# A fused attention backward pass on one core: block-end transposes behind the dK products, VectorE's block-end work behind its 32x32 transposes, and the dQ copy on VectorE

## The chip, the cores and the metric

The kernel runs on one core of one Trainium2 chip. The metric is device time in microseconds (us) for one execution. Each kernel was timed in several runs, on the same chip as runs of the kernel before, and every comparison uses fast runs only: those within 1.5% of the kernel's fastest. The engine names are those of the profile: PE does the matrix products, PEld loads their weights, DVE is VectorE, ACT is ScalarE, POOL is GpSimd. A trace line such as "L720 ACT ACTIVATE eT<-sps" is the instruction of line 720 of that kernel on ScalarE, reading the tensor `sps` and writing `eT`.

## The reference

The reference returns the output of two attention blocks and all gradients of their inputs. Nearly all the time that matters here goes to block B, multi-query attention with 16 heads of 28 channels over 2,048 tokens, one shared K and V:

```python
def _B_ref(x, wq, wk, wv, wo):
    ...
    q = (x @ wq) -> (B, H, S, Dh);  k = x @ wk;  v = x @ wv       # shortened
    scores = einsum("bhqd,bkd->bhqk", q, k) * Dh ** -0.5
    p = softmax(scores, axis=-1)
    o = einsum("bhqk,bkd->bhqd", p, v)
    return o.transpose(...).reshape(B, S, H * Dh) @ wo

def reference(..., grad_out):
    out, vjp = jax.vjp(forward, ...)      # forward = concat(block A, block B)
    return (out, *vjp(grad_out))
```

## The kernel before

The core of the kernel is one loop over 512 *units*. A unit is 256 keys by 256 queries for two heads; 8 units make a *block* (all keys for one query chunk and two heads), and there are 64 blocks. Forward and backward are interleaved: in iteration `u`, PE makes the scores of unit `u`, the gradients of the probabilities of unit `w = u-16`, the output products of unit `v = u-1`, the dQ products of unit `y = u-18`, and the dK products of a block that began 28 units ago. All engines run the program in this order, each its own instructions.

```python
psS = tile_pool("psS", bufs=3, space=PSUM)    # score buffers, name "sps"
psD = tile_pool("psD", bufs=2, space=PSUM)    # gradient buffers, name "dps"
oq     = psA.tile([P, 512], F32, name="oq")   # columns 0:256: O in rows 0:64, dQ in rows 64:128
dk_acc = psA.tile([P, 512], F32, name="dk_acc")
...
for u in range(NU + 28):
    sp = [psS.tile([P, 512], F32, name="sps") for _ in range(2)]
    dp = [psD.tile([P, 512], F32, name="dps") for _ in range(2)]
    rows_SD(u, sp, dp)                        # PE: scores, gradients (four 32-row groups side by side)

    nc.scalar.activation(et[:, u % 2, 0, :], sp[0], Exp, scale)              # L710 "first exponential"
    nc.vector.tensor_tensor(dst[:, 0, :], dp[0], ew[:, w % 2, 0, :], mult)   # L715 VectorE's product
    nc.scalar.activation(cp, dp[1], Copy)                                    # L717
    nc.gpsimd.tensor_tensor(dst[:, 1, :], cp, ew[:, w % 2, 1, :], mult)      # L718
    nc.scalar.activation(et[:, u % 2, 1, :], sp[1], Exp, scale)              # L720 "second exponential"
    ...
    if (u - 9) % 8 == 0:     # block end, unit 1 of a block (cut)
        onp = psS.tile([P, 2, 2, 32], F32, name="sps")
        nc.tensor.transpose(onp..., oTs[b]...)                               # L731
        nc.vector.reciprocal(r_, onp[..., 0:1])                              # L740
        nc.vector.tensor_tensor(onat..., onp, r_, mult)                      # L744
        ...
    if (u - 14) % 8 == 0:    # unit 6
        tp2 = psS.tile([P, 1024], BF16, name="sps")
        nc.tensor.transpose(tp2..., don[b]...)                               # L776
        nc.vector.tensor_copy(doT[b]..., tp2...)                             # L780
    # dK products of block (u-28)//8: 12 matmuls a unit, 8 in two units, none in two
    # output products (v) and dQ products (y) into oq; dV products in units 2 and 3
    ...
    if u % 64 in (16, 24) and u > 64:
        out_proj(...)        # four products into a score buffer, copied out by VectorE
    if v % 8 == 7:           # unit 0
        nc.vector.tensor_copy(oTs[v // 8], oq[0:64, 0:256])                  # L844
    if y % 8 == 7:           # unit 1: the dQ copy
        nc.scalar.activation(qT_B..., oq[64:128, 0:256], Copy, scale)        # L847
    nc.vector.transpose(dsx[b][:, tp]..., dsT[y]...)                         # L853, 32x32 transposes
```

Three score buffers serve two scores a unit, so the buffers rotate: a score product can start when the last reader of the buffer that it is given is done. Which buffer a tile gets is settled when the program is built. Mostly it is the one used three allocations earlier. The block-end transposes take a turn in the same rotation, and there it depends on the order of the program around them: at unit 7 of this kernel the second score tile gets the buffer of the transpose just before it, which the `doT` copy frees.

## Time and profile before

| | before |
|---|---|
| median of 3 runs, ahead of the prediction | 1173.73 us (1172.52 to 1174.92) |
| span of the profiled run | 1172.0 us |
| ordinary block (41 of blocks 8 to 62), median | 12.78 us |
| block with an output projection (14 of them), median | 13.74 us |
| first exponential to first exponential, units 0 to 7 of an ordinary block | 1.458, 2.026, 1.457, 1.519, 1.458, 1.545, 1.811, 1.506 us |
| second exponential to next first, unit 1 to 2 and unit 6 to 7 | 1.056 us and 0.841 us |

A block is measured from the start of its first exponential to that of the next block. A unit needs at least 1.458 us on ScalarE; what a unit takes above that is what there is to win or lose.

The first line of the page, busy time of each engine over the whole span:

```profile
PE 1099.7 (94%) x15388; PEld 444.6 (38%) x15388; DVE 885.5 (76%) x1669; ACT 900.9 (77%) x1788; POOL 699.4 (60%) x835
```

PE looks like the limit. The groups of instructions of ScalarE between 400 and 1000 us say otherwise (columns: line, engine, operation, tensors, shapes, count, then busy us and mean ns, then idle time just before and what ended it):

```profile
L720 ACT ACTIVATE eT<-sps 128x512 bf16<-128x512 f32 x369 | 224.8, 609 | 0.0
L710 ACT ACTIVATE eT<-sps 128x512 bf16<-128x512 f32 x369 | 221.5, 600 | 18.1 <-PE dps L591 16.6
...
L847 ACT ACTIVATE R_63<-oq 64x256 bf16<-64x256 f32 x46 | 17.4, 379 | 5.0 <-PE oq L591 4.1
```

The Trainium skill, "Trainium Kernel Development and Optimization", Performance Expectations, warns of just this reading of matmul busy time, and here the warning holds. In 600 us ScalarE is idle for about 23 us. Its instructions are the pace, and the first exponential is the only one that waits to speak of. The passage from unit 1 to unit 2, in the timeline (columns: start us, length us, then the instruction):

```profile
676.32 0.62 ACT L720 ACTIVATE eT<-sps 128x512 bf16<-128x512 f32 x1
...
676.66 0.59 PE L591 MATMUL sps<-R_63,R_65 32*128 32x256 bf16 x2
...
676.96 0.38 ACT L847 ACTIVATE R_63<-oq 64x256 bf16<-64x256 f32 x1
...
677.00 0.36 PE L591 MATMUL sps<-R_63,R_65 32*128 32x256 bf16 x2
...
677.37 0.60 ACT L710 ACTIVATE eT<-sps 128x512 bf16<-128x512 f32 x1
```

The dQ copy ends at 677.34, and the last score product of unit 2 ends at 677.36. The copy and the scores are ready at the same moment, 1.05 us after the second exponential began. The scores are late because their buffer is the one that the second exponential reads until 676.94.

The passage from unit 6 to unit 7, in the timeline of the same kernel:

```profile
683.45 0.27 PE L776 MATMUL sps<-identB,don 128*64 128x128 bf16 x2
...
683.95 0.27 DVE L780 COPY doT<-sps 64x256 bf16<-64x256 bf16 x1
684.15 0.69 DVE L853 STREAM_TRANSPOSE dsx<-dsT 128x512 f32<-128x512 f32 x1
684.32 0.60 ACT L720 ACTIVATE eT<-sps 128x512 bf16<-128x512 f32 x1
...
684.74 0.28 PE L591 MATMUL sps<-R_63,R_65 32*128 32x256 bf16 x2
...
685.16 0.60 ACT L710 ACTIVATE eT<-sps 128x512 bf16<-128x512 f32 x1 [0.24 <-PE dps L591]
```

Here the score products of unit 7 start at 684.74, while the second exponential still runs (to 684.92): they do not need its buffer. The `doT` copy, ahead of VectorE's 32x32 transpose, has freed theirs by 684.22. The step is 0.84 us, and it is PE's queue that sets it.

The waits of PE between 400 and 1000 us show one wait for VectorE (columns: instruction and what it waited for, us in total, times, longest):

```profile
PE sps L731 <- DVE oTs L844: 8.2, 12, 0.7
```

### The profile page before, as it was taken

What the parts mean: (1) busy time and instruction counts of PE and PEld (TensorE: products, weight loads), DVE (VectorE), ACT (ScalarE), POOL (GpSimd) and SP (SyncE); (2) the same over time, 40 slices, a digit from 0 to 9 for tenths busy, and PEclk for the clock granted to TensorE, in tenths of its full rate; (3) what the DMA queues carried; (4) which work ended last, traced back from release to release, by engine and by line L of the source; (5) the groups of instructions that cost most, each with busy time, mean ns of one, the idle gap of its engine ahead of it and who ended that gap; (6) DMA issues with size and microseconds to landing.
All of it is one profiled execution on the core that took longest, in us unless ns stands there. A gap on an engine that the chain in (4) does not pass through costs nothing. (4 is left out here: it accounts for less than half of the span.)

```text
span 1172.0 us, 38434 instructions
## 1 busy us (share of the span) xinstructions
PE 1099.7 (94%) x15388; PEld 444.6 (38%) x15388; DVE 885.5 (76%) x1669; ACT 900.9 (77%) x1788; POOL 699.4 (60%) x835
## 2 busy tenths in 40 slices
PE   7999997988989999999999999999999999999998
PEld 4555543333333333333333333333333333333344
DVE  7886400336889898888889888988999899888922
ACT  3453112357989999999999999999999999999511
POOL 9000150003777777777778777877787778777900
PEclk9999998989999999999999999999999999999999
DMA  9779897059999999999999999999999999999962
GB/s 259 126 130 184 160 188 177 20 125 198 180 179 190 188 164 187 190 184 175 189 188 160 199 188 186 162 198 188 152 195 182 189 170 199 184 168 163 240 147 75
DMA packets 684435, 202.91 MB, mean 173 GB/s; under 512 B 651232, under 2 KB 679392, under 8 KB 684256
## 3 DMA queue, kind: packets, MB, share of 16 engines
q1 hardware_dynamic: 673664, 190.26, 94.8%
q10 hardware_dynamic: 9312, 6.65, 2.1%
q0 software_dynamic: 1280, 3.55, 1.1%
q8 instruction: 120, 1.97, 0.7%
q14 instruction: 59, 0.48, 0.1%
HBM read 22.83 MB, written 15.03 MB: 32 GB/s over the span
## 5 line engine op out<-in xcount | busy, mean ns | idle before, releaser
L718 POOL TENSOR_TENSOR dsT<-cp,eT 128x512 bf16<-128x512 bf16 x512 | 590.3, 1153 | 193.2 <-ACT cp L717 156.2
L715 DVE TENSOR_TENSOR dsT<-dps,eT 128x512 bf16<-128x512 f32 x512 | 347.8, 679 | 58.3 <-PE dps L591 37.6
L853 DVE STREAM_TRANSPOSE dsx<-dsT 128x512 f32<-128x512 f32 x512 | 357.8, 699 | 1.3 <-POOL dsT L718 0.3
L710 ACT ACTIVATE eT<-sps 128x512 bf16<-128x512 f32 x512 | 307.3, 600 | 42.2 <-PE dps L591 28.3
L591 PEld LDWEIGHTS <-R_65 32*128 32x128 bf16 (+1 forms) x8192 | 171.5, 92 | 403.3 <-issue 356.1
L717 ACT ACTIVATE cp<-dps 128x512 bf16<-128x512 f32 x512 | 305.1, 596 | 12.0 <-PE dps L591 11.1
L720 ACT ACTIVATE eT<-sps 128x512 bf16<-128x512 f32 x512 | 311.6, 609 | 0.0
L591 PE MATMUL dk_acc<-dsx,qX 32*32 32x512 bf16 x4096 | 290.4, 377 | 0.0
L591 PE MATMUL dps<-doT,R_65 32*128 32x256 bf16 x2048 | 253.9, 271 | 7.7 <-DVE R_64 L824 1.1
L591 PE MATMUL sps<-R_63,R_65 32*128 32x256 bf16 x2048 | 242.9, 276 | 5.9 <-ACT eT L710 2.0
L591 PE MATMUL oq<-eT,R_65 128*32 128x256 bf16 x2048 | 213.8, 278 | 2.5 <-issue 0.3
L591 PE MATMUL oq<-dsT,R_65 128*32 128x256 bf16 x2048 | 203.1, 278 | 1.1 <-POOL dsT L718 0.9
L591 PEld LDWEIGHTS <-qX 32*32 32x32 bf16 x4096 | 69.4, 89 | 94.1 <-issue 54.1
L591 PE MATMUL dv_acc<-eN,don 128*32 128x512 bf16 x1024 | 86.9, 382 | 2.5 <-DMA eN<-eT 2.5
L521 DVE TENSOR_TENSOR osb<-R_65 32x512 bf16<-32x512 bf16 x4 | 1.7, 413 | 74.2 <-ACT R_65 L518 74.2
L380 POOL MEMSET ga<- 64x448 bf16 x2 | 0.9, 468 | 90.8 <-PE agen L337 71.3
L553 POOL MEMSET R_65<- 128x16 bf16 x1 | 0.2, 172 | 70.8 <-DVE R_65 L552 70.8
L748 POOL TENSOR_TENSOR don<-R_64,rl 128x128 bf16<-128x128 bf16 x64 | 25.8, 403 | 21.4 <-DVE rl L740 21.4
L844 DVE COPY oTs<-oq 64x256 f32<-64x256 f32 x64 | 26.5, 414 | 15.1 <-PE oq L591 14.4
L731 PE MATMUL sps<-identF,oTs 64*128 64x64 f32 x128 | 21.3, 247 | 17.0 <-DVE oTs L844 10.6
L591 PEld LDWEIGHTS <-don 128*32 128x32 bf16 x1024 | 34.7, 97 | 4.0 <-issue 3.9
L79 PEld LDWEIGHTS <-R_64 128*128 128x128 bf16 x256 | 23.9, 100 | 28.0 <-issue 10.3
(216 smaller groups left out, 961.2 us busy)
## 6 DMA issues: line engine op xcount, KB each, us to landing
qX<-qn_d SPq DMA_DIRECT2D x128, 64.0 KB
out_dram<-osb ACTq DMA_DIRECT2D x44, 112.0 KB
eN<-eT SPq DMA_TRANSPOSE x256
qn_d<-dsx SPq DMA_DIRECT2D x1, 2048.0 KB
on_d<-onat SPq DMA_DIRECT2D x8, 256.0 KB
xa<-in_A_x_dram SPq DMA_DIRECT2D x8, 224.0 KB
ga<-in_grad_out_dram SPq DMA_DIRECT2D x4, 448.0 KB
xa<-in_grad_out_dram POOLq DMA_DIRECT2D x4, 448.0 KB, 4.7
```

Of the source, the lines that this page charges most:

```text
L79: nc.tensor.matmul(out_ap, lhsT=lhsT, rhs=rhs, start=start, stop=stop, tile_position=(0, 0))
L521: nc.vector.tensor_tensor(out=sq[0:32, :], in0=kT[0:32, qc * 512:(qc + 1) * 512], in1=kT[0:32, qc * 512:(qc + 1) * 512], op=ALU.mult)
L591: nc.tensor.matmul(out, lhsT=lhsT, rhs=rhs, start=start, stop=stop, tile_position=pos, skip_group_check=True)
L710: nc.scalar.activation(out=et[:, u % 2, 0, :], in_=sp[0][:, :], func=ACT.Exp, scale=scale)
L715: nc.vector.tensor_tensor(out=dst[:, 0, :], in0=dp[0][:, :], in1=ew[:, w % 2, 0, :], op=ALU.mult)
L717: nc.scalar.activation(out=cp[:, :], in_=dp[1][:, :], func=ACT.Copy)
L718: nc.gpsimd.tensor_tensor(out=dst[:, 1, :], in0=cp[:, :], in1=ew[:, w % 2, 1, :], op=ALU.mult)
L720: nc.scalar.activation(out=et[:, u % 2, 1, :], in_=sp[1][:, :], func=ACT.Exp, scale=scale)
L731: nc.tensor.transpose(onp[:, qb, :, :].rearrange("p h c -> p (h c)"), oTs[b][0:64, qb * P:(qb + 1) * P], identF[0:64, 0:64], tile_position ...
L748: nc.gpsimd.tensor_tensor(out=dn[:], in0=dnv, in1=r_[:].to_broadcast([P, 2, 2, 32]), op=ALU.mult)
L844: nc.vector.tensor_copy(out=oTs[v // 8][:, :], in_=oq[0:64, 0:256])
L853: nc.vector.transpose(out=dsx[b][:, tp, :, :, :].rearrange("p h t c -> p (h t c)").bitcast(F32), in_=dsT[y][:, :, :].rearrange("p h c -> p ...
```

## The change

The intent is to shorten three waits at block ends. PE runs the dK products first and the block-end transposes after them, so that it has work while their inputs come. VectorE puts the 32x32 transpose ahead of the block-end work, so that the pacing chain's buffers come free earlier. The dQ copy leaves ScalarE, the pacer. The diff moves the pieces into helper functions; the new order is its core:

```diff
 # PE
-    onat_T(b)      at u % 8 == 1    # the helpers' names are used for the moved code
-    don_T(b)       at u % 8 == 6
-    dK products
+    dk_units(u)
+    onat_T(b)      at u % 8 == 1
+    don_T(b)       at u % 8 == 6
     output and dQ products, dV products
 ...
 # VectorE (GpSimd's parts move with it)
-    reciprocal, normalisation       (u % 8 == 1, ahead of the projection's copy)
-    row sums                        (u % 8 == 4)
-    doT copy                        (u % 8 == 6)
-    oTs copy                        (u % 8 == 0)
     32x32 transpose
+    o_norm(b): reciprocal, normalisation
+    row_D(b):  row sums
+    don_copy(b)
+    oTs copy
+    dQ copy
 ...
-    nc.scalar.activation(out=qT_B[g][64 * hp:64 * hp + 64, qc * 256:(qc + 1) * 256],
-                         in_=oq[64:128, 0:256], func=ACT.Copy, scale=scale)
+    nc.vector.tensor_scalar(out=qT_B[g][64 * hp:64 * hp + 64, qc * 256:(qc + 1) * 256],
+                            in0=oq[64:128, 0:256], scalar1=scale, scalar2=None, op0=ALU.mult)
```

In the kernel after, the first exponential is L827, VectorE's product L832, ScalarE's gradient copy L834, GpSimd's product L835, the second exponential L837, the two block-end transposes L697 and L741, the `doT` copy L749, the 32x32 transpose L876, the `oTs` copy L893 and the dQ copy L896.

## The prediction

> **What bounds the kernel.** The loop over 512 units (8 units make a block, 64 blocks) fills about 840 of 1172 us. The page shows PE 94% busy, but the Trainium skill, "Trainium Kernel Development and Optimization", Performance Expectations, warns that matmul busy time is a bad metric since matmuls are pipelined; the timeline agrees: groups of four 0.28 us matmuls start 0.12 us apart. In the timeline ScalarE is the pacer: its three activations per unit follow each other start to start in 0.493, 0.477 and 0.488 us, 1.458 us a unit, and 8 x 1.458 = 11.66 of the 12.78 us of an ordinary block. The rest: 0.57 at unit 1 (dQ copy 0.41, and 0.15 before it), 0.35 at unit 6, 0.2 of small delays. Blocks with an output projection (14) take 13.74 us. VectorE is busy about 89% (stretches of the windows view), GpSimd waits for ScalarE (view of waits).
>
> **What the change does.** It removes the dQ copy (0.38 us, x64) from ScalarE, adds it to VectorE (about 0.42 us, as the similar oTs copy), lets PE run the dK products while the transposes' inputs come, and puts VectorE's block end one 32x32 transpose (0.62 us start to start) later.
>
> **Why I expect no gain.** PE is in order, and three score buffers rotate. After each block-end transpose the next unit's scores need the buffer of the second exponential.
> - Unit 1 to 2: the score matmul starts 0.05 us after that exponential ends (0.617 us long), and the next exponential follows about 0.38 us after that start: about 1.045 us from start to start. Today exponential plus dQ copy take 1.054. The copy sits in a gap that exists anyway: gain 0.01 us a block.
> - Unit 6 to 7: today the scores take the doT transpose's buffer, released by VectorE's early doT copy, and the step is 0.841 us. With that copy after the 32x32 transpose, the built program's waits show the scores of unit 7 waiting for the second exponential of unit 6 instead: about 0.995 us. Loss 0.15, and about 0.06 more at unit 7, where PE arrives late. The reordering on PE gains 0.1 us there, which this wait hides.
> - Output-projection blocks: VectorE runs late there (it waits 1.07 us for the projection). Its chain of projection copy, transpose, oTs, product, transpose, reciprocal, normalisation, dQ copy now ends about 0.9 us after today's dQ copy; PE's output products of unit 2 wait for it, and with them the scores of unit 3: about 0.65 us more a block.
>
> Sum (estimate from the durations above): 50 x 0.2 + 14 x 0.9 = 23 us, all on the pacing loop; I shade it slightly for gains I can't see.
>
> **Predicted: 1194 us, range 1178 to 1204.** Chances: faster 0.06, same 0.55, slower 0.39.
>
> **What would show it.** Ordinary block about 12.98 us (right) or under 12.6 (wrong). ScalarE's busy time falls by about 24 us but its idle time before the first exponential rises by more. The step unit 6 to 7 grows from 0.84 to about 1.0; unit 1 to 2 stays near 1.04. PE's wait for the oTs copy at the first transposes shrinks in ordinary blocks; waits for the dQ copy appear on PE in projection blocks. VectorE busy rises about 25 us.
>
> **What would make it wrong.** If the scores' release is faster than 0.05 us or PE arrives later than I think; if the earlier VectorE products release the gradient buffers so that ScalarE's small delays vanish (0.2 us a block, 13 us); if the dQ copy on VectorE is much shorter than 0.42 us.

## The result, and the profile after

Ratios here and below are taken from the fast runs of the same rounds; they are not quite the ratio of the medians that are quoted.

| | before | after |
|---|---|---|
| median of fast runs, 4 of each in the same rounds | 1174.33 us (1172.52 to 1181.33) | 1203.66 us (1202.06 to 1206.16) |
| ratio, 95% interval | | 1.0243 (1.021 to 1.0275): slower |
| span of the profiled run | 1172.0 us | 1200.7 us |
| ordinary block, median | 12.78 us | 13.01 us (mean 13.02) |
| projection block, median | 13.74 us | 14.61 us (mean 14.89) |
| unit 1 to 2, unit 6 to 7 | 1.056, 0.841 us | 1.054, 0.991 us |
| VectorE, ScalarE busy | 885.5, 900.9 us | 911.7, 883.9 us |

The work moved as meant. The first line of the page after:

```profile
PE 1100.5 (92%) x15388; PEld 440.8 (37%) x15388; DVE 911.7 (76%) x1733; ACT 883.9 (74%) x1724; POOL 701.6 (58%) x835
```

ScalarE does 64 instructions and 17 us less, and the kernel is slower. Its groups in the same 600 us tell where the time went:

```profile
L837 ACT ACTIVATE eT<-sps 128x512 bf16<-128x512 f32 x355 | 215.1, 606 | 0.0
L827 ACT ACTIVATE eT<-sps 128x512 bf16<-128x512 f32 x356 | 213.5, 600 | 56.3 <-PE sps L591 17.5 <-issue 16.5 <-PE dps L591 13.6
```

The idle time before the first exponential went from 18.1 to 56.3 us, and 355 units pass where 369 did. Unit 1 to 2 in the timeline after:

```profile
756.15 0.62 ACT L837 ACTIVATE eT<-sps 128x512 bf16<-128x512 f32 x1
...
756.30 0.28 PE L591 MATMUL sps<-R,R 32*128 32x256 bf16 x1
...
756.82 0.26 PE L591 MATMUL sps<-R,R 32*128 32x256 bf16 x1 [0.24 <-ACT eT L837]
...
757.04 0.42 DVE L896 TENSOR_SCALAR R<-oq 64x256 bf16<-64x256 f32 x1
...
757.21 0.60 ACT L827 ACTIVATE eT<-sps 128x512 bf16<-128x512 f32 x1 [0.44 <-issue]
...
757.52 0.29 PE L591 MATMUL oq<-eT,R 128*32 128x256 bf16 x2 [0.30 <-DVE R L896]
```

The copy is gone from ScalarE and the step is the same: the scores wait for the second exponential, start 0.05 us after its end, and the next exponential follows 0.39 us later. ("issue" means that the profile shows nothing that ended the idle time; the scores end at 757.19.) Unit 6 to 7 in the timeline after:

```profile
763.88 0.30 PE L741 MATMUL sps<-identB,don 128*64 128x128 bf16 x2
763.90 0.70 DVE L876 STREAM_TRANSPOSE dsx<-dsT 128x512 f32<-128x512 f32 x1
...
764.19 0.60 ACT L837 ACTIVATE eT<-sps 128x512 bf16<-128x512 f32 x1
...
764.44 0.67 PE L591 MATMUL sps<-R,R 32*128 32x256 bf16 x2
...
764.63 0.29 DVE L749 COPY doT<-sps 64x256 bf16<-64x256 bf16 x1
...
764.85 0.28 PE L591 MATMUL dps<-doT,R 32*128 32x256 bf16 x2
...
765.18 0.60 ACT L827 ACTIVATE eT<-sps 128x512 bf16<-128x512 f32 x1 [0.39 <-PE sps L591]
```

The first score group begins at 764.44 but takes 0.67 us, since one of its matmuls cannot start before the second exponential ends at 764.79; all behind it start at 764.85. PE reached the scores 0.25 us after the second exponential began, 0.17 us earlier than before (0.42), and that is of no use. PE takes its products strictly in order, as the Trainium skill, "TensorE: Matmul & The Clock Gate", Part 3, The mechanism, states (strict order of arrival), and this trace agrees: the gradient products, whose own waits were over by 764.30 (VectorE's product and ScalarE's copy of unit 6), start with the blocked scores at 764.85. The scores do not wait for the `doT` copy here, which ends only at 764.92.

Projection blocks have a larger loss. Before, timeline at units 1 to 3 of one of them:

```profile
703.49 0.38 ACT L847 ACTIVATE R_63<-oq 64x256 bf16<-64x256 f32 x1 [0.37 <-PE oq L591]
...
703.90 0.60 ACT L710 ACTIVATE eT<-sps 128x512 bf16<-128x512 f32 x1
...
703.92 0.29 PE L591 MATMUL oq<-eT,R_65 128*32 128x256 bf16 x2
...
705.36 0.60 ACT L710 ACTIVATE eT<-sps 128x512 bf16<-128x512 f32 x1
```

After, the timeline of the same block:

```profile
715.90 0.60 ACT L827 ACTIVATE eT<-sps 128x512 bf16<-128x512 f32 x1 [0.78 <-POOL dsT L835]
...
716.40 0.43 DVE L896 TENSOR_SCALAR R<-oq 64x256 bf16<-64x256 f32 x1
...
716.88 0.29 PE L591 MATMUL oq<-eT,R 128*32 128x256 bf16 x2 [1.06 <-DVE R L896]
...
718.08 0.60 ACT L827 ACTIVATE eT<-sps 128x512 bf16<-128x512 f32 x1 [0.60 <-PE dps L591]
```

The copy comes last in VectorE's queue at a block end, PE's output products wait 1.06 us for it, and unit 2 takes 2.18 us instead of 1.46 us. The waits of PE after, between 400 and 1000 us:

```profile
PE oq L591 <- DVE R L896: 22.0, 44, 1.1
PE sps L697 <- DVE oTs L893: 8.4, 11, 0.8
PE sps L591 <- ACT eT L837: 8.2, 34, 0.2
```

The first and the third line are new. The wait for the dQ copy is there in ordinary blocks too, 0.30 us each (at 757.52 in the trace above).

One more thing is new. In 4 of the 14 projection blocks PE runs at half its clock for 3.413 us, and those blocks take 15.6 us instead of 14.6. The windows view after, around one of them (columns: stretch, length, busy us with counts of PE, PEld, DVE, ACT and POOL, granted PE clock, DMA share, GB/s):

```profile
497.00:500.50 3.50, 1.66 (x38) 0.87 (x34) 3.40 (x8) 2.72 (x6) 1.87 (x3) 1.00 0.86 203
500.50:504.00 3.50, 3.50 (x48) 1.03 (x44) 2.60 (x5) 2.21 (x6) 2.39 (x3) 0.52 0.48 96
```

PE is busy for less than half of the stretch before the drop. Before, there is no such window in the loop between 311 and 1170 us.

The sum, from the two profiled runs: 41 ordinary blocks x 0.242 = 9.9 us; 10 projection blocks x 0.86 and 4 with a slow clock x 1.85, together 14 x 1.14 = 16.0 us; the first eight blocks +0.4; ahead of the loop -0.5; from block 63 to the end +2.9. That is 28.7 us, as the spans differ.

### The profile page after: what moved, and what is told of

Read it like the earlier page. It is cut to its first block, busy times and chain, and to the rows that moved or that the text cites. A ratio compares the mean times of both kernels' runs of the same rounds, so it can differ in the third digit from the quotient of the medians.

```text
span 1200.7 us, 38383 instructions
## 1 busy us (share of the span) xinstructions
PE 1100.5 (92%) x15388; PEld 440.8 (37%) x15388; DVE 911.7 (76%) x1733; ACT 883.9 (74%) x1724; POOL 701.6 (58%) x835
## 5 line engine op out<-in xcount | busy, mean ns | idle before, releaser
L835 POOL TENSOR_TENSOR dsT<-cp,eT 128x512 bf16<-128x512 bf16 x512 | 591.2, 1155 | 215.2 <-ACT cp L834 203.0
L832 DVE TENSOR_TENSOR dsT<-dps,eT 128x512 bf16<-128x512 f32 x512 | 353.1, 690 | 77.9 <-ACT eT L837 40.4
L827 ACT ACTIVATE eT<-sps 128x512 bf16<-128x512 f32 x512 | 307.0, 600 | 91.0 <-PE sps L591 35.3
L876 DVE STREAM_TRANSPOSE dsx<-dsT 128x512 f32<-128x512 f32 x512 | 358.7, 701 | 0.0
L591 PEld LDWEIGHTS <-R 32*128 32x128 bf16 (+1 forms) x8192 | 171.6, 93 | 407.1 <-issue 387.2
L834 ACT ACTIVATE cp<-dps 128x512 bf16<-128x512 f32 x512 | 304.2, 594 | 16.7 <-PE dps L591 16.7
L837 ACT ACTIVATE eT<-sps 128x512 bf16<-128x512 f32 x512 | 310.0, 606 | 0.0
L591 PE MATMUL dk_acc<-dsx,qX 32*32 32x512 bf16 x4096 | 293.8, 381 | 0.0
L591 PE MATMUL sps<-R,R 32*128 32x256 bf16 x2048 | 250.9, 277 | 22.3 <-ACT eT L837 11.7
L591 PE MATMUL dps<-doT,R 32*128 32x256 bf16 x2048 | 241.2, 274 | 5.1 <-DVE R L858 1.1
L591 PE MATMUL oq<-eT,R 128*32 128x256 bf16 x2048 | 212.7, 280 | 29.5 <-DVE R L896 29.1
L591 PE MATMUL oq<-dsT,R 128*32 128x256 bf16 x2048 | 205.3, 281 | 2.4 <-DVE R L896 1.8
L79 PEld LDWEIGHTS <-R 128*128 128x128 bf16 (+1 forms) x416 | 34.2, 99 | 36.3 <-issue 12.3
L718 POOL TENSOR_TENSOR don<-R,rl 128x128 bf16<-128x128 bf16 x64 | 25.9, 404 | 26.8 <-ACT eT L827 23.1
L79 PE MATMUL agen<-R,R 128*128 128x448 bf16 x128 | 29.8, 363 | 3.2 <-DVE pk L227 1.9
L697 PE MATMUL sps<-identF,oTs 64*128 64x64 f32 x128 | 21.4, 248 | 11.6 <-DVE oTs L893 10.7
```

The source lines that it names most:

```text
L79: nc.tensor.matmul(out_ap, lhsT=lhsT, rhs=rhs, start=start, stop=stop, tile_position=(0, 0))
L591: nc.tensor.matmul(out, lhsT=lhsT, rhs=rhs, start=start, stop=stop, tile_position=pos, skip_group_check=True)
L697: nc.tensor.transpose(onp[:, qb, :, :].rearrange("p h c -> p (h c)"), oTs[b][0:64, qb * P:(qb + 1) * P], identF[0:64, 0:64], tile_position ...
L718: nc.gpsimd.tensor_tensor(out=dn[:], in0=dnv, in1=r_[:].to_broadcast([P, 2, 2, 32]), op=ALU.mult)
L827: nc.scalar.activation(out=et[:, u % 2, 0, :], in_=sp[0][:, :], func=ACT.Exp, scale=scale)
L832: nc.vector.tensor_tensor(out=dst[:, 0, :], in0=dp[0][:, :], in1=ew[:, w % 2, 0, :], op=ALU.mult)
```

## The experiments

The theory T is that of the prediction: at unit 7 the rotation of the score buffers ties the scores to the second exponential; in projection blocks VectorE's late dQ copy holds PE. The main rivals are R1: only VectorE's added work counts, each of its microseconds costs one; and R2: what hurts is PE's new order. Twelve kernels ran besides the two, all of them compared with the kernel before on the same chip; three gave wrong outputs, as told there, and nine correct ones.

| run | ordinary block | projection block, median | span | median | ratio to before, 95% |
|---|---|---|---|---|---|
| before | 12.78 | 13.74 | 1172.0 | 1174 | |
| after | 13.01 | 14.61 | 1200.7 | 1203.66 | 1.0243 (1.021 to 1.0275) |
| a_dq_scalar | 12.98 | 13.95 | 1186.1 | 1187.53 | 1.0093 (1.0066 to 1.0121) |
| b_dq_vector | 13.02 (mean) | 14.39 | 1191.7 | 1195.14 | 1.0153 (1.0127 to 1.0179) |
| b_dk_first | 12.98 | 13.88 | 1183.7 | 1185.83 | 1.0091 (1.0046 to 1.0136) |
| b_block_end_late | 12.98 | 14.50 | 1193.2 | 1194.99 | 1.0175 (1.0127 to 1.0223) |
| b_dot_late | 12.98 | 13.89 | 1184.0 | 1188.44 | 1.0139 (1.0097 to 1.0181) |
| a_dq_first | 12.98 | 14.49 | 1197.2 | 1198.62 | 1.0207 (1.0182 to 1.0232) |
| a_extra | 13.56 | 15.59 | 1230.9 | 1234.43 | 1.0509 (1.0485 to 1.0534) |
| a_extra2 | 13.43 | 15.48 | 1224.7 | 1226.49 | 1.0451 (1.0415 to 1.0486) |
| a_own (wrong outputs) | 12.63 | 14.30 | 1180.4 | 1182.44 | 1.0079 (1.0055 to 1.0103) |
| a_own_dqs (wrong outputs) | 12.84 | 14.56 | 1203.0 | 1194.52 | 1.0189 (1.0143 to 1.0236) |
| a_own_mix (wrong outputs) | 12.63 | 14.56 | 1179.6 | 1182.97 | 1.0106 (1.0057 to 1.0156) |
| best | 12.89 | 14.99 | 1199.3 | 1200.11 | 1.0202 (1.0165 to 1.024) |

All times are in us. The block figures come from the profiled run, the medians from the timed runs.

### One part undone: a_dq_scalar

The changed kernel with the dQ copy back on ScalarE:

```diff
-    nc.vector.tensor_scalar(out=qT_B..., in0=oq[64:128, 0:256], scalar1=scale, ..., op0=ALU.mult)
+    nc.scalar.activation(out=qT_B..., in_=oq[64:128, 0:256], func=ACT.Copy, scale=scale)
```

> The changed kernel with the dQ copy back on ScalarE, all else as changed. Buffer theory (the scores of units 2 and 7 wait for the second exponential of the unit before, so ScalarE has a gap of about 0.5 us there that the copy fits into; VectorE's copy hurts only where VectorE is late, in the projection blocks): ordinary block stays near 12.96 us, projection block falls from 14.6 to about 13.95, total about 1191 us. Rival, VectorE load (64 copies of 0.427 us are 27 us, just the size of the loss): all of the loss goes, about 1176 us, ordinary block near 12.78.

Measured: 1187.53 us. A projection block fell from 14.61 to 13.95 us (median), so the copy on VectorE costs 0.66 us there; the prediction had about 0.65. An ordinary block fell only from 13.01 to 12.98: 0.20 of the 0.23 us that ordinary blocks lost are not the copy's. No half-clock window is left in blocks 8 to 62.

### One part alone: b_dq_vector, b_dk_first, b_block_end_late

Three kernels with one part of the change each in the kernel before: the dQ copy on VectorE in its old place; only PE's order; only VectorE's order.

```diff
 # b_dq_vector: before, the same line as above the other way round
-    nc.scalar.activation(out=qT_B..., func=ACT.Copy, scale=scale)
+    nc.vector.tensor_scalar(out=qT_B..., scalar1=scale, op0=ALU.mult)
 # b_dk_first: before
+    dk_units(u)
     onat_T(b) / don_T(b), each followed at once by its VectorE work as in before
-    dk_units(u)
 # b_block_end_late: before
-    o_norm, do_o, row_D, don_copy, oTs and dQ copies ahead of the 32x32 transpose
     nc.vector.transpose(...)
+    o_norm, do_o, row_D, don_copy, oTs and dQ copies
```

> The kernel before with only the dQ copy moved to VectorE. Buffer theory: nearly nothing in ordinary blocks (12.78 stays, unit 1 to 2 stays near 1.05 us), about 0.3 us more in each of 14 projection blocks, total about 1178 us. Rival, VectorE load: plus 27 us, about 1201 us.

> The kernel before with only PE's order changed: dK products ahead of the block-end transposes. The built program then has the scores of unit 7 wait for the second exponential of unit 6. Buffer theory: step unit 6 to 7 from 0.84 to about 0.99, unit 7 plus 0.06, ordinary block about 12.98, total about 1187 us. Rival, VectorE load: no work is added to VectorE, so 1174 us.

> The kernel before with only VectorE's block end put behind its 32x32 transposes; dQ on ScalarE and PE's order as before. The built program has the same wait at unit 7 as the changed kernel. Buffer theory: ordinary block about 12.98, projection blocks about 0.8 us longer, since PE waits for the later oTs copy ahead of the dK products: total about 1195 us. Rival, VectorE load: 1174 us, as no work is added.

The first expectation missed: b_dq_vector came at 1195.14 us, well above what the theory had, and below what the rival had. Its timeline at unit 2 shows why:

```profile
740.15 0.43 DVE L847 TENSOR_SCALAR R<-oq 64x256 bf16<-64x256 f32 x1
...
740.61 0.71 DVE L853 STREAM_TRANSPOSE dsx<-dsT 128x512 f32<-128x512 f32 x1
...
740.65 0.60 ACT L710 ACTIVATE eT<-sps 128x512 bf16<-128x512 f32 x1 [0.44 <-issue]
...
741.36 0.69 DVE L715 TENSOR_TENSOR dsT<-dps,eT 128x512 bf16<-128x512 f32 x1
```

In the old order the copy stands ahead of the 32x32 transpose, and with both ahead of it VectorE's product of unit 2 starts 0.71 us after the first exponential (before: 0.09). That product frees a gradient buffer, which the gradients of unit 3 need, so unit 2 takes 1.65 to 1.77 us instead of 1.46. The step from unit 1 to 2 did not shorten here either: 740.65 - 739.60 = 1.05. Taking the dQ copy off ScalarE gains nothing, shown in two orders; what it costs depends on what stands behind it on VectorE.

The other two each lengthened the ordinary block to 12.98 us, the same sum as almost the whole change, and with the same step from unit 6 to 7, 0.99 us. So the parts do not add: either one alone brings the new tie at unit 7. In both built programs, as in the changed one, the scores of unit 7 wait for both exponentials of unit 6, and in the program before they wait for the first and for the `doT` copy. R2 alone does not hold, since b_block_end_late keeps PE's old order. On projection blocks b_block_end_late is bad (14.50), and PE's new order takes most of that back: a_dq_scalar, which is both parts together, has 13.95. In b_block_end_late PE waits 1.30 us for the `oTs` copy in a projection block, and two of the 14 have a half-clock window, although the dQ copy is on ScalarE there: these windows are not tied to that copy.

### The rotation alone: b_dot_late

In the kernel before, one swap on VectorE: the `doT` copy goes behind the 32x32 transpose of its unit. The order on every other engine is unchanged, and so is the work.

```diff
                                             tile_position=(0, r))
-                    doT[b] = pw_.tile([P, 256], BF16, name="doT")
-                    nc.vector.tensor_copy(out=doT[b][r:r + 64, :], in_=tp2[r:r + 64, 0:256])
 ...
                 nc.vector.transpose(...)
+                if u >= 14 and (u - 14) % 8 == 0 and (u - 14) // 8 < NB:
+                    ...
+                    nc.vector.tensor_copy(out=doT[b][r:r + 64, :], in_=tp2[r:r + 64, 0:256])
```

> The kernel before with one pair of VectorE instructions per block swapped: in unit 6 the doT copy comes behind the 32x32 transpose. The instructions of all engines are the same, and so is the order on PE, ScalarE and GpSimd; but the scores of unit 7 now get the second exponential's buffer. Buffer theory: step unit 6 to 7 from 0.84 to 0.99 us, unit 7 plus 0.05, every block 0.2 us longer (ordinary 12.98, projection 13.94), total about 1187 us. If the loss of the changed kernel's ordinary blocks comes from VectorE's work or from PE's order: 1174 us.

Measured: 1188.44 us, ordinary block 12.98, step from unit 6 to 7 0.991 us. Its timeline there:

```profile
757.03 0.60 ACT L720 ACTIVATE eT<-sps 128x512 bf16<-128x512 f32 x1
...
757.42 0.29 DVE L858 COPY doT<-sps 64x256 bf16<-64x256 bf16 x1
...
757.45 0.50 PE L591 MATMUL sps<-R,R 32*128 32x256 bf16 x2
...
757.70 0.28 PE L591 MATMUL dps<-doT,R 32*128 32x256 bf16 x2
...
758.03 0.60 ACT L710 ACTIVATE eT<-sps 128x512 bf16<-128x512 f32 x1 [0.39 <-PE sps L591]
```

The picture is that of the changed kernel: a first score group stretched to 0.50 us, the rest started at 757.70, 0.07 us after the second exponential's end. No work was added to VectorE, nothing moved on PE. One displaced copy of 0.29 us costs 0.20 us a block, so it is the place in the rotation that is paid for.

### The order inside VectorE's block end: a_dq_first

The changed kernel with the dQ copy directly behind the 32x32 transpose, ahead of the reciprocal and the normalisation:

```diff
                 nc.vector.transpose(...)
+                if 0 <= y < NU and y % 8 == 7:
+                    nc.vector.tensor_scalar(out=qT_B..., in0=oq[64:128, 0:256], ...)
                 if (b := due(u, 9)) is not None:
                     o_norm(b)
 ...
-                if 0 <= y < NU and y % 8 == 7:
-                    nc.vector.tensor_scalar(out=qT_B..., in0=oq[64:128, 0:256], ...)
```

> The changed kernel with the dQ copy moved ahead of the reciprocal and the normalisation on VectorE; the same instructions. Theory of waits: the output products of unit 2 start about 0.4 us sooner; ordinary block 12.97 us (from 13.02), projection block about 0.3 us shorter than 14.6, total about 1197 us. VectorE load: 1204 us.

Measured: 1198.62 us. Unit 2 of an ordinary block is back at 1.457 us from 1.504, so the late copy did cost 0.05 us there, a small cost that the prediction did not have. A projection block fell by 0.12 us only, not the 0.3 expected: most of the lateness there is what stands ahead on VectorE, not the reciprocal and the normalisation.

### Work added on VectorE: a_extra and a_extra2

Useless work in unit 5 on a tensor that is no longer read, to see what a microsecond of VectorE costs:

```diff
                     don_copy(b)
+                if u % 8 == 5 and 8 <= v < NU:
+                    o2 = oTs[v // 8 - 1]
+                    nc.vector.tensor_tensor(out=o2[:, :], in0=o2[:, :], in1=o2[:, :], op=ALU.mult)
+                    nc.vector.tensor_scalar(out=o2[:, :], in0=o2[:, :], scalar1=scale, scalar2=None, op0=ALU.mult)
 # a_extra2: two tensor_scalar instead
```

> The changed kernel with two useless VectorE instructions (some 0.4 to 0.5 us, on a spent tile) in unit 5 of each block, where VectorE has slack. Rival, VectorE load: each us of VectorE work costs a us, so plus about 25 to 30 us, about 1230 us. Theory of waits (only where VectorE's work stands in front of something PE or ScalarE waits for does it cost): no change, 1204 us, ordinary block 13.02 us.

> The changed kernel with two useless VectorE instructions of the one-input kind in unit 5 of each block (0.284 us each in the run before, so about 0.5 us a block start to start, more than the dQ copy). VectorE load: 64 x 0.5 us, plus about 32 us, 1235 us. Theory of waits: it only pushes the products of unit 6 by less than their slack of about 0.44 us, so ordinary block stays within 0.1 us of 13.02, total 1204 to 1209 us.

Measured: 1234.43 and 1226.49 us. Both miss what the theory expected (1204, and 1204 to 1209), and the first is about what R1 expected; but the additions were not short. The groups of VectorE in a_extra, 500 to 1000 us:

```profile
L893 DVE TENSOR_TENSOR oTs<-oTs 64x256 f32<-64x256 f32 x36 | 45.8, 1272 | 0.0
...
L894 DVE TENSOR_SCALAR oTs<-oTs 64x256 f32<-64x256 f32 x36 | 10.2, 284 | 1.2
```

The first probe was three times the length I had put down for it. The Trainium skill, "SBUF — State Buffer", Who interferes with whom, states that VectorE with two operands in SBUF, or in a two-port mode, shares an exclusive port pair with GpSimd, and that the loser waits. GpSimd's products fill most of that time, and the trace agrees: in one block of a_extra the tensor_tensor starts at 767.19 during a product of GpSimd that ends at 768.18, and itself ends at 768.46, 0.28 us later. The same tensor_scalar takes 0.284 us behind the tensor_tensor; in a_extra2 the first of the two takes 1.12 us on average and the second 0.28. So the probes were not small: they added 92 and 84 us of VectorE's instruction time over the kernel, for 30.2 and 24.0 us of span. A microsecond of VectorE thus cost about 0.3 us. R1's rate of one to one is wrong, but the additions were not free either: the products of unit 6 came late and with them the gradient scores of unit 7. A clean test of a short harmless addition was not made and stays open.

### The rotation taken away: a_own, a_own_dqs, a_own_mix

These take the block-end transposes out of the rotation: both write to the spare half of `oq`.

```diff
         def onat_T(b):
-            onp = psS.tile([P, 2, 2, 32], F32, name="sps")
+            onp = oq[:, 256:384].rearrange("p (q h c) -> p q h c", q=2, h=2)
 ...
-            tp2 = psS.tile([P, 1024], BF16, name="sps")
+            tp2 = oq[:, 384:512].bitcast(BF16)
 # a_own_dqs: as a_own, dQ copy on ScalarE
 # a_own_mix: as a_own, dQ copy on ScalarE in projection blocks only
```

> The changed kernel with the two block-end transposes written to the unused half of the output accumulator's bank, so that they take no score buffer, and no scores wait for the second exponential of the unit before in ordinary blocks. Buffer theory: step unit 1 to 2 from 1.05 to about 0.65 us, step unit 6 to 7 from 0.99 to about 0.72, unit 7 back to about 0.53; but the dQ copy on VectorE, no longer behind a gap, then holds PE at unit 2 for about 0.3 us; ordinary block about 12.58 us, total about 1175 us. Rival, VectorE load: its work is the same, so 1204 us.

> The same with the dQ copy on ScalarE. Buffer theory: unit 1 to 2 is then second exponential plus copy with no gap, about 0.90 us; ordinary block about 12.5 us, projection block about 13.5, total about 1157 us, faster than both kernels. Rival, VectorE load: as the changed kernel with dQ on ScalarE, 1187 us.

> The same with the dQ copy on ScalarE in projection blocks and on VectorE elsewhere. Buffer theory: ordinary block as in a_own (12.58), projection block as in a_own_dqs (13.5), total about 1161 us. If the copy on VectorE does not hold PE at unit 2, this is the fastest, about 1150 us.

All three gave wrong results (relative error 1.24 in a_own). The Trainium skill, "PSUM — Partial Sum Buffer", The four PSUM rules, states that a product that opens a group clears the accumulation marks of a whole bank in the rows that it writes, so that two groups open there at once spoil each other without an error; the transposes fell into the middle of the sums of O and dQ in the same bank. No run isolates that, but the wrong outputs agree, and the form in the next experiment, which opens a group there only in the first and the last block, was correct. The timing stands as a test of the waits, since the amount of work on every engine is that of the changed kernel. The timeline of a_own from unit 6 to 7:

```profile
742.18 0.60 ACT L837 ACTIVATE eT<-sps 128x512 bf16<-128x512 f32 x1
...
742.43 0.28 PE L591 MATMUL sps<-R,R 32*128 32x256 bf16 x2
...
742.86 0.60 ACT L827 ACTIVATE eT<-sps 128x512 bf16<-128x512 f32 x1
```

The scores run under the second exponential and the step is 0.68 us. An ordinary block takes 12.63 us, 0.38 less than the changed kernel and 0.15 less than the kernel before; the total is 20 us below the changed kernel with the same VectorE work (988 against 989 us of instruction time). That is the strongest evidence against R1. The step from unit 1 to 2 falls to 0.63 us in a_own too, but the block does not gain by it, as the waits of PE between 400 and 1000 us show:

```profile
PE oq L591 <- DVE R L896: 39.9, 46, 1.1
```

PE's output products now wait about 0.80 us for the dQ copy in an ordinary block, and unit 2 takes 1.92 us instead of 1.50. Units 1 and 2 together take 3.51 us, against 3.53 in the changed kernel and 3.48 in the kernel before. What a_own gains, it gains at units 6 and 7: 3.16 us, against 3.52 and 3.32. In a_own_dqs the step from unit 1 to 2 is 1.28 us, since ScalarE's copy also had to wait for VectorE's normalisation, which now reads the same tile, so the two do not compare the copy's place alone. a_own_dqs and a_own_mix missed the 1157 and 1161 us expected of them, and a_own_mix, 1182.97 us, did not beat a_own. (The profiled run of a_own_dqs lost some 10 us ahead of the loop, so its span is not compared.)

### A correct version with the rotation gone: best

```diff
-            onp = psS.tile([P, 2, 2, 32], F32, name="sps")
+            onp = oq[:, 256:384]...
-                nc.tensor.transpose(onp[:, qb]..., oTs[b]..., identF[0:64, 0:64], tile_position=(0, 0))
+                mmt(onp[:, qb]..., oTs[b]..., identF[0:64, 0:64], (0, 0), b == 0 and qb == 0, True)
 # the other transpose likewise, into oq[:, 256:512]
             nc.vector.tensor_copy(out=doT[b]..., in_=tps2.pop(b)...)
+            nc.vector.memset(oq[r:r + 64, 256:384], 0.0)
 # and the dQ copy ahead of o_norm, as in a_dq_first
```

> The changed kernel with the block-end transposes in the accumulator's spare columns, now as plain products[...], a small clearing write by VectorE, and the dQ copy ahead of the normalisation. Buffer theory: step unit 1 to 2 about 0.62 us, unit 2 to 3 about 0.55, unit 6 to 7 about 0.68; ordinary block about 12.25 us, projection block about 13.9; total about 1150 us, faster than both kernels although VectorE does some 20 us more work than in the changed kernel. VectorE load: 1220 us or more.

Measured: correct, 1200.11 us, 2.0% slower than before. It was expected at about 1150 us and missed that by 50. The first block-end transpose as a plain f32 product took 0.58 us of PE's queue instead of 0.26 (each of its two products shows as two matmul records; the other transpose, of bf16, took no longer), and the `doT` copy out of f32 0.42 us instead of 0.27. The slower transpose stands ahead of the scores of unit 2, and the step from unit 1 to 2 is 0.95 us instead of a_own's 0.63. The output products of unit 2 then wait 0.72 us for the normalisation, which reads the same tile, and unit 2 takes 1.84 us. Seven half-clock windows fell into blocks 8 to 62, and one came just after. No version that I tried with correct results beats the kernel before.

## Why the prediction was right or wrong

**"Taking the dQ copy off ScalarE gains 0.01 us a block": right.** The step from unit 1 to 2 is 1.056 us with the copy and 1.054 without. b_dq_vector shows the same with nothing else changed, and a_own shows the condition: take the rotation away, and the step falls to 0.63 us (though unit 2 then gives it back, waiting for the copy on VectorE).

**"Unit 6 to 7 grows from 0.84 to about 1.0": right, 0.991 us.** The mechanism is shown by b_dot_late, which reproduces it by one displaced copy, and by a_own, which removes it. The 0.06 us at unit 7 came as 0.05. PE's new order gained nothing there.

**"0.2 us an ordinary block": right, 0.24.** The missing 0.04 is the copy's small cost at unit 2, which a_dq_first takes away; the prediction had PE waiting for the copy in projection blocks only, and it waits 0.30 us in ordinary ones too.

**"0.9 us a projection block": the term that was too small; it measured 1.14.** The mechanism was right. The copy ended 0.92 us later in the block, against "about 0.9", and a_dq_scalar gives 0.66 us for what it costs, against "about 0.65". Ten undisturbed blocks lost 0.86 us each. (Before, the copy ends at 703.87 in a block that begins at 699.45, after at 716.83 in one that begins at 711.49.) What was not foreseen are the half-clock windows in 4 of the 14 blocks, about 1 us each. They come where PE waits 1.06 us for the dQ copy, and none is left in blocks 8 to 62 of a_dq_scalar, where that wait is gone; b_block_end_late has two behind another wait of PE. What rule of the clock brings them was not tested.

**The total.** The prediction's sum was 23 us, shaded to 20; the spans differ by 28.7. The parts come to 28.7 against 22.6 us, so 6.1 are missing: 3.4 in projection blocks (16.0 against 12.6), 2.9 from block 63 to the end, and -0.2 in all the rest, where ordinary blocks are fewer than the 50 put down but dearer. The end contains a half-clock stretch of 6.8 us. In the other traces it takes 93.96 to 95.09 us without such a stretch and 95.08 to 96.02 with one of 3.4 us, against 97.09 here, so the loss goes with the slow clock, but no run isolates it. Shading a sum for gains that could not be named was the wrong way: none came. The measured 1203.66 us lies 0.34 us inside the upper edge of the range, and two of the four runs lie beyond it: that the total fits is partly luck. The prediction also held "same" (0.55) likelier than "slower" (0.39), and slower it was.

**The signs named.** ScalarE's busy time fell by 17 us, not 24, although the 64 copies of 0.379 us are 24 us: its instructions overlap in the records (0.60 us long, 0.49 us apart), the busy view counts overlapped time once, and where units stand further apart less of it overlaps; its idle time before the first exponential rose by 38 us in 600, as said. VectorE's rose by 26, against 25. The wait for the dQ copy appeared on PE. PE's wait for the `oTs` copy did not shrink, 8.2 and 8.4 us in the view of waits: 12 and 11 waits in a stretch that holds 11 projection blocks, so there was little to shrink in ordinary ones. That sign was wrong.

## What to carry to other kernels

When an instruction leaves the pacing engine, look first at what the next instruction of that engine would be waiting for at that moment: here the score products were ready 0.02 us after the copy ended, and there was nothing to gain. When buffers rotate through a pool, an extra user of the pool changes which reader the next product waits for, and so does any move that makes one reader finish earlier or later than another; read those waits off the built program for every order you consider. The engine that looks half idle still sets release times: put the copy that PE waits for ahead of the one that nobody waits for.

## What the Trainium skill lacked or had wrong

- "TensorE: Matmul & The Clock Gate", Part 1 ties the half rate to an idle window of about 3.4 us, and Why this matters asks to avoid gaps of more than about 3 us. Part 1 also tells of a second failure mode, frequent short idles, without a measure for it. Here the clock was halved in four projection blocks for 3.413 us each, a length that agrees, after gaps of at most 1.07 us, and in the run called best eight times with no gap above 0.87 us. In the aligned 3.41 us ahead of each of the four, PE was busy by its records for 1.64 to 1.70 us. Over the traces of all runs, between 362 and 1135 us, drops followed windows of 1.57 to 2.54 us busy, and windows down to 2.03 us passed without one. The measurement decides: gaps of about 1 us in a window half busy are enough in this case, and the records give no sharp bound.
- What such a window costs in a kernel that ScalarE paces has no place on that page: about 1 us in a block of 14.6 us here, although PE ran at half its rate for 3.4 us.
- "SBUF — State Buffer", Who interferes with whom, has the rule for VectorE and GpSimd but no times for it, only two ratios without shapes: a 64x256 f32 tensor_tensor with both inputs in SBUF took 1.27 us while GpSimd was working, and a tensor_scalar 0.28 or 1.12 us by its place.
- "PSUM — Partial Sum Buffer", The four PSUM rules, does not say what the way around costs: an f32 transpose made as two plain products that open no group took 0.58 us instead of 0.26.
